# Two load queues, idle transposes, a second PSUM bank and another order of weight loads in a fused threshold-attention and MoE kernel

## Chip, cores, metric

One core of a Trainium2 chip. The metric is device microseconds of one execution. A trace covers the span from the first to the last instruction, which lies 1.8 us under the time of the same execution. "Mean clock" is the share of TensorE's full clock that the chip granted, averaged over the span; a "dip" is a stretch at half of it. One dip of 3.41 us takes 0.003 off the mean; half speed after the last matmul counts too, and takes up to 0.002.

## The reference

```python
def _attn_ref(q, k, v, tau):                 # q, k, v: (8, 8, 576, 64)
    scores = np.matmul(q, k.transpose(0, 1, 3, 2)) / np.sqrt(64)
    thresh = np.max(scores, axis=-1, keepdims=True) - tau
    scores = np.where(scores >= thresh, scores, -1000000000.0)
    attn = softmax(scores)
    return np.matmul(attn, v)
# heads side by side: x is (4608, 512)
def _moe_ref(x, w_in, w_out):                # (512, 2048), (2048, 512)
    h = x @ w_in
    return (h * np.clip(h + 3.0, 0.0, 6.0) / 6.0) @ w_out
```

## The kernel before

Heads come in quads (four heads, 16 quads), a quad in nine slots of score rows, so 144 slots. In each slot VectorE takes the row maximum out of PSUM, GpSimd makes a bias of it, ScalarE masks and takes the exponential, GpSimd normalizes, and a transpose (by DMA, or in early odd slots by TensorE) makes the operand for the product with v. From slot 23 on, pieces of the MoE run between the slots. What stands behind other work in an engine's line has to wait for it (the prediction shows GpSimd's bias behind three loads). The weights are loaded by GpSimd, in loads that also convert them to bf16. A bank, below, is a buffer in PSUM, the memory that TensorE writes its results to: the next product into it waits until it has been emptied.

```python
    N1 = 22
    N2 = 28
    ...
    def bank(name):                       # for transposes and products with v
        nonlocal turn
        turn += 1
        if now < N2 and turn % 2:
            return ps_o.tile([P, 512], F32, tag="o", name=name)   # ps_o: one bank, later MoE's
        return ps_m.tile([P, 512], F32, tag="m", name=name)       # ps_m: one bank
    ...
    def warm_up(count):                   # idle transposes: nobody reads the result
        warm = ps_h.tile([P, 2, 512], F32, tag="h", name="warm")
        for _ in range(count):
            nc.tensor.transpose(warm[:, 0, 0:P], identf[:], identf[:])
    ...
    transpose_rest(0)()                   # last of k and q of the first quad
    ...
    for n, sl in enumerate(queue):        # the slots
        ...
        if prev is not None:
            for i in range(2):
                sm_exp(prev, i)           # ScalarE
        sm_max(sl)                        # VectorE maximum, GpSimd bias
        ...                               # a piece of the MoE, reciprocal of prev
        for i in range(2):
            sm_mask(sl, i)                # ScalarE, waits for the bias
        ...                               # transposes, products with v
        if n + 1 < len(queue):
            queue[n + 1].tiles = scores(queue[n + 1].quad, queue[n + 1].slot)
        if n < 8:
            warm_up(6)
        if prev is not None:
            sm_norm(prev)                 # GpSimd
        flush()
        late.extend(outs)
        start(loads, 1)                   # q and k, on SyncE
        if n < 4 or n > 12:
            start(vcasts, 1)              # v, on GpSimd
        if n > 3:
            start(casts, 1 if n < 24 else 2)   # weights, on GpSimd
```

Of the kernel before, what the change touches and what calls it, by code (L numbers as in the profile page):

```python
# [9 lines left out]
F32 = mybir.dt.float32  # L10
# [3 lines left out]
Act = mybir.ActivationFunctionType  # L14

P = 128
# [5 lines left out]
def kernel(  # L22
# [10 lines left out]
    nc = tc.nc  # L33
    B, H, S, D = q.shape
    assert (B, H, S, D) == (8, 8, 576, 64)
    d_model, d_ff = moe_w_in.shape
# [4 lines left out]
    NSLOT = 9  # L41
    NB = 2
    N1 = 22
    N2 = 28
    scale = 1.0 / math.sqrt(D)
    tau = float(tau)

# [12 lines left out]
    o_pool = ctx.enter_context(tc.tile_pool(name="op", bufs=3))  # L60
# [14 lines left out]
    casts = []  # L75
# [4 lines left out]
    def load_quad(quad):  # L80
        b, g = divmod(quad, 2)
        nat[quad] = (nat_pool.tile([P, 1152], F32, tag="nq", name="nq"),
                     nat_pool.tile([P, 4, 4, D], F32, tag="km", name="km"),
                     nat_pool.tile([P, 2 * D], F32, tag="kr", name="kr"))
        nq, km, kr = nat[quad]

        def main(dst, src, h, order):
            nc.sync.dma_start(out=dst[:, :, h, :], in_=src[b, 4 * g + h, 0:512, :].rearrange(order, t=4))

        def blocks_q(n, a, j):  # L90
            c = 32 * (2 * a + j)
            nc.sync.dma_start(out=nq[c:c + 32, n * S:(n + 1) * S].rearrange("p (k d) -> p k d", d=32),
                              in_=q[b, 4 * g + 2 * n + a, :, 32 * j:32 * j + 32].rearrange("(k r) d -> r k d", r=32))

        def load_q(n):
            if b < NB:
                for a in range(2):
                    main(nq[:, 0:1024].rearrange("p (t h d) -> p t h d", h=4, t=4), q, 2 * n + a, "(t p) d -> p t d")
            else:
                for a in range(2):  # L100
                    for j in range(2):
                        blocks_q(n, a, j)

        def rest():
            for dst, src in ((kr[:], k), (nq[:, 1024:1152], q))[0:2 if b < NB else 1]:
                for n in range(2):
                    nc.sync.dma_start(out=dst[64 * n:64 * n + 64, :].rearrange("p (h d) -> p h d", h=2),
                                      in_=src[b, 4 * g + 2 * n:4 * g + 2 * n + 2, 512:S, :].rearrange("h p d -> p h d"))

        for n in range(2):  # L110
            loads.append(lambda n=n: [main(km, k, 2 * n + a, "(p t) d -> p t d") for a in range(2)])
            loads.append(lambda n=n: load_q(n))
            if n == 0:
                loads.append(rest)
# [34 lines left out]
    def start(jobs, n):  # L149
        for _ in range(min(n, len(jobs))):  # L150
            jobs.pop(0)()
# [9 lines left out]
    def warm_up(count):  # L161
# [3 lines that stand above are left out]
# [34 lines left out]
    def copy_out(out, in_):  # L199
        if 0 <= now < N1:  # L200
            nc.vector.tensor_copy(out=out, in_=in_)
        else:
            nc.scalar.copy(out=out, in_=in_)  # L203


    def by_pe(pair):
        return pair // NPAIR < NB
# [16 lines left out]
    def transpose_k(pair):  # L224
        ps = main_pe(nat[pair // 2][1], pair)
        return lambda: copy_out(kT_of(pair)[:, 64:576], ps[:])

    def transpose_rest(quad):
        ps = bank("tr")
        nq, _, kr = nat[quad]  # L230
        nc.tensor.transpose(ps[:, 0:P], kr[:], identf[:])
        if by_pe(2 * quad):
            nc.tensor.transpose(ps[:, P:2 * P], nq[:, 1024:1152], identf[:])

        def evict():
            qT, kT = qkT[quad]
            both = ps[:].rearrange("p (w n t) -> p w n t", n=2, t=64)
            if by_pe(2 * quad):
                nc.vector.tensor_copy(out=qT[:, :, 512:S], in_=both[:, 1])
            copy_out(kT[0:64, :, S:S + 64], both[0:64, 0])  # L240
            copy_out(kT[64:P, :, 0:64], both[64:P, 0])
        return evict

    def keys(pair, a, hf):
# [140 lines left out]
    def mm2_out(bb, mt, on_act):  # L385
        osb = o_pool.tile([P, d_model], F32, tag="osb", name="osb")
        if on_act:
            nc.scalar.activation(out=osb[:], in_=o_ps[0], func=Act.Copy, scale=1.0 / 6.0)  # L388
        else:
            nc.vector.tensor_scalar_mul(out=osb[:], in0=o_ps[0], scalar1=1.0 / 6.0)  # L390
        b0 = 2 * bb * S
        if mt == 4:
            return [(osb[0:64, :], out[b0 + 512:b0 + S, :]), (osb[64:P, :], out[b0 + S + 512:b0 + 2 * S, :])]
        r0, t = (b0, mt) if mt < 4 else (b0 + S, mt - 5)
        return [(osb[:], out[r0 + t * P:r0 + (t + 1) * P, :])]
# [23 lines left out]
    evict_q = transpose_q(0)  # L419
    evict()  # L420
    evict_q()
    transpose_rest(0)()

    queue = []
    for quad in range(NQUAD):
# [8 lines left out]
    for n, sl in enumerate(queue):  # L434
        quad, slot = sl.quad, sl.slot
        b, g = divmod(quad, 2)
        now = n
        if slot in (0, 4):
            pts[2 * quad + slot // 4] = pt_pool.tile([P, 9, 512], BF16, tag="pT", name="pT")
        if slot == 8:  # L440
            ptr[quad] = ptr_pool.tile([P, 9, P], BF16, tag="pR", name="pR")
        if quad == 0 and slot == 0:
            load_quad(1)
        if slot == (4 if quad else 8) and quad + 2 < NQUAD:
            load_quad(quad + 2)
        if slot == 0 and g == 1 and b + 1 < B:
            load_v(b + 1)
        if prev is not None:
            for i in range(2):
                sm_exp(prev, i)  # L450
        sm_max(sl)

        if slot != 8 and todo1:
            item, then = todo1.pop(0)
            h = mm1(item)
            r = mm1_relu(h, on_act=(slot in (0, 1, 3, 5)))
            mm1_gate(item, h, r)
            todo2.extend(then)
        copies = pe_transpose(queue[n - 2]) if n > 1 and queue[n - 2].on_chip else None
        if prev is not None:  # L460
            sm_recip(prev)
        if copies:
            copies()
        outs = []


        pieces = 0 if slot == 3 else 1
        if slot == 0:
            second = True
        if second and slot < 2 and len(todo2) > 1 and todo2[0][1] == todo2[1][1]:  # L470
            pieces, second = 2, False
        for _ in range(pieces):
            if todo2:
                bb, mt, part = todo2.pop(0)
                mm2_part(bb, mt, part)
                if part == 3:
                    outs += mm2_out(bb, mt, on_act=False)
        for i in range(2):
            sm_mask(sl, i)
        evict = None  # L480
        nxt = 2 * quad + 2
        if slot == (1 if quad else 2):
            evict = transpose_q(2 * quad + 1)
        elif slot == (2 if quad else 3):
            evict = transpose_k(2 * quad + 1)
        elif slot == 3 and quad > 0:
            av_main(2 * quad - 1)
        elif slot == 4 and quad > 0:
            av_rest(quad - 1)
            if quad % 2 == 0:  # L490
                todo1.extend(moe_of(quad // 2 - 1))
        elif slot in (5, 6, 7) and quad + 1 < NQUAD:
            if slot == 5:
                alloc_qk(quad + 1)
                evict = transpose_q(nxt)
            elif slot == 6:
                evict = transpose_k(nxt)
            else:
                evict = transpose_rest(quad + 1)
        elif slot == 8:  # L500
            av_main(2 * quad)
        if evict:
            evict()
        if n + 1 < len(queue):
            queue[n + 1].tiles = scores(queue[n + 1].quad, queue[n + 1].slot)
        if n < 8:
            warm_up(6)
        if prev is not None:
            sm_norm(prev)
        flush()  # L510
        late.extend(outs)
        start(loads, 1)
        if n < 4 or n > 12:
            start(vcasts, 1)
        if n > 3:
            start(casts, 1 if n < 24 else 2)
        prev = sl

    for i in range(2):
# [3 lines left out]


    last = NQUAD - 1
    count = [0, 0]

    def rest1(item, then):
        h = mm1(item, pool=ps_s if count[0] % 3 else None)
# [4 lines left out]
    def rest2():  # L534
        while todo2:
            bb, mt, part = todo2.pop(0)
            mm2_part(bb, mt, part, pool=ps_s if count[1] % 3 else None)
            if part == 3:
                flush()
                late.extend(mm2_out(bb, mt, on_act=(count[1] % 2 == 0)))  # L540
                count[1] += 1

    for item in todo1:
# [42 lines left out]
```

## Time and profile before

| | |
|---|---|
| three runs before the prediction | 561.0, 561.12, 562.59 us |
| the run that was profiled | 564.1 us (span 562.3, mean clock 0.989) |
| first mask, third, fourth (ScalarE, slots 0, 2, 3) | 10.72, 18.23, 21.31 us |
| mask of slot 14, of slot 31 | 54.80, 112.25 us |

The start of ScalarE's mask is a good milestone: one per slot, in order, on an engine that is 90% busy from 25 to 109 us (75.62 of 84 us). Compare two traces by the difference of these starts, slot by slot; it stays constant where nothing changed and steps where something did. The lines are in the prediction.

### The profile page before, as it was taken

What the parts mean: (1) busy time and instruction counts of PE and PEld (TensorE: products, weight loads), DVE (VectorE), ACT (ScalarE), POOL (GpSimd) and SP (SyncE); (2) the same over time, 40 slices, a digit from 0 to 9 for tenths busy, and PEclk for the clock granted to TensorE, in tenths of its full rate; (3) what the DMA queues carried; (4) which work ended last, traced back from release to release, by engine and by line L of the source; (5) the groups of instructions that cost most, each with busy time, mean ns of one, the idle gap of its engine ahead of it and who ended that gap; (6) DMA issues with size and microseconds to landing.
All of it is one profiled execution on the core that took longest, in us unless ns stands there. A gap on an engine that the chain in (4) does not pass through costs nothing.

```text
span 562.3 us, 11634 instructions
## 1 busy us (share of the span) xinstructions
PE 535.0 (95%) x3856; PEld 309.3 (55%) x3856; DVE 424.4 (75%) x1040; ACT 470.3 (84%) x999; POOL 305.2 (54%) x646
## 2 busy tenths in 40 slices
PE   7998798899999999999999999999999999999997
PEld 5665455455545565555555565655555565654663
DVE  3588787687878788787878798887978798883440
ACT  4799899798988999989898999899898999983540
POOL 1678878854556555655456555755556555561000
PEclk8899999899999999999999999999999999999999
DMA  5879999997689876978589867987699865453102
GB/s 110 135 110 166 162 160 184 207 148 144 112 159 153 151 153 127 208 139 155 114 150 170 159 137 146 174 160 146 127 137 175 167 124 117 101 109 86 38 20 75
DMA packets 286204, 77.52 MB, mean 138 GB/s; under 512 B 269248, under 2 KB 281536, under 8 KB 286144
## 3 DMA queue, kind: packets, MB, share of 16 engines
q1 hardware_dynamic: 268736, 67.86, 64.8%
q0 software_dynamic: 17408, 8.92, 13.7%
q8 instruction: 30, 0.49, 0.4%
q14 instruction: 30, 0.25, 0.2%
HBM read 36.70 MB, written 9.44 MB: 82 GB/s over the span
## 4 chain that ended last, share of the span: by engine, by line
PE 58%; DVE 11%; ACT 9%; issue 4%; POOL 1%; DMA 1%; SPq 1%; DVEq 0%; POOLq 0%
PE h L353 18%; PE o L382 17%; PE s L256 16%; DVE s L277 5%; ACT s L285 4%; PE av L323 3%; ACT s L290 3%; DVE g L370 2%; DVE r L364 2%; ACT r L362 2%; PE s L262 1%; PE tp L213 1%; PE ar L323 1%; DVE osb L390 1%; POOL pn L298 1%
## 5 line engine op out<-in xcount | busy, mean ns | idle before, releaser
L298 POOL TENSOR_SCALAR pn<-s,rinv 128x576 bf16<-128x576 f32 x288 | 211.6, 745 | 133.5 <-issue 58.5
L277 DVE TENSOR_SCALAR_CACHE_REDUCE s<-s 128x576 f32<-128x576 f32 x288 | 205.9, 752 | 44.9 <-PE s L256 35.2
L285 ACT ACTIVATE s<-s,bias 128x576 f32<-128x576 f32 x288 | 207.1, 766 | 36.8 <-POOL bias L280 35.7
L290 ACT ACTIVATE s<-s 128x576 f32<-128x576 f32 x288 | 192.7, 671 | 0.3
L256 PE MATMUL s<-kT,qT 64*128 64x288 f32 x1024 | 172.7, 435 | 5.4 <-DVE s L277 3.2
L353 PE MATMUL h<-xT,w_in_sb 128*128 128x320 bf16 (+1 forms) x1024 | 145.0, 287 | 5.5 <-DVE g L370 4.6
L382 PE MATMUL o<-w_out_sb,g 128*128 128x512 bf16 x576 | 140.9, 379 | 3.6 <-DVE osb L390 3.0
L353 PEld LDWEIGHTS <-w_in_sb 128*128 128x128 bf16 x1024 | 92.0, 97 | 68.4 <-issue 31.1
L256 PEld LDWEIGHTS s<-kT,qT 64*128 64x128 f32 x1024 | 94.8, 188 | 62.7 <-DVE s L277 24.9
L370 DVE SCALAR_TENSOR_TENSOR g<-r,h 128x512 bf16<-128x512 f32 (+1 forms) x128 | 96.4, 754 | 41.2 <-ACT r L362 39.3
L280 POOL TENSOR_SCALAR bias<-m 128x1 f32<-128x1 f32 x288 | 54.4, 189 | 69.0 <-DVE s L277 48.2
L382 PEld LDWEIGHTS <-g 128*128 128x128 bf16 x576 | 55.6, 98 | 58.2 <-issue 9.8
L362 ACT ACTIVATE r<-h,three 128x640 f32<-128x640 f32 (+1 forms) x74 | 54.4, 737 | 21.1 <-PE h L353 20.4
L290 ACT ACTIVATION_READ_ACCUMULATOR s<-s 128x1 f32 x288 | 54.2, 188 | 0.0
L364 DVE TENSOR_SCALAR r<-h 128x512 f32<-128x512 f32 (+1 forms) x54 | 40.5, 751 | 0.0
L390 DVE TENSOR_SCALAR osb<-o 128x512 f32<-128x512 f32 x31 | 21.0, 676 | 22.2 <-PE o L382 22.2
L323 PE MATMUL av<-pT,vm 128*64 128x512 bf16 x256 | 34.6, 392 | 2.0 <-ACT kT L203 2.0
L323 PEld LDWEIGHTS <-vm 128*64 128x64 bf16 x512 | 18.1, 111 | 25.2 <-issue 18.3
L293 DVE RECIPROCAL rinv<-rsum 128x2 f32<-128x2 f32 x144 | 23.0, 160 | 10.2 <-ACT s L290 9.5
L335 DVE CAST xT<-av 128x512 bf16<-128x512 f32 x32 | 21.8, 681 | 5.6 <-PE av L326 5.3
L277 DVE DVE_READ_ACCUMULATOR s<-s 128x1 f32 x288 | 23.9, 83 | 0.0
L388 ACT ACTIVATE osb<-o 128x512 f32<-128x512 f32 x5 | 3.0, 597 | 23.9 <-PE o L382 23.9
(42 smaller groups left out, 255.9 us busy)
## 6 DMA issues: line engine op xcount, KB each, us to landing
km<-in_k_dram SPq DMA_DIRECT2D x64, 128.0 KB, 3.0
out_dram<-osb SPq DMA_DIRECT2D x32, 256.0 KB, 2.4
nq<-in_q_dram SPq DMA_DIRECT2D x96, 72.0 KB, 2.7
vm<-in_v_dram POOLq DMA_DIRECT2D x16, 256.0 KB, 5.4
nq<-in_q_dram SPq DMA_DIRECT2D x16, 128.0 KB, 3.9
w_in_sb<-in_moe_w_in_dram POOLq DMA_DIRECT2D x16, 128.0 KB, 4.1
w_out_sb<-in_moe_w_out_dram POOLq DMA_DIRECT2D x16, 128.0 KB, 4.5
pT<-pn SPq DMA_TRANSPOSE x119, 3.4
```

The costliest lines, as they stand in the source:

```text
L256: nc.tensor.matmul(tiles[a][:, hf, 0:HALF], qT_of(pair)[a * 64:(a + 1) * 64, t * P:(t + 1) * P], keys(pair, a, hf), start=True, stop=True)
L277: nc.vector.tensor_scalar(out=sl.s[:, i, :].rearrange("p (a b) -> p a b", a=2), in0=ps[:, :, 0:HALF], scalar1=1.0, scalar2=None, op0=Alu.m ...
L280: nc.gpsimd.tensor_scalar(out=sl.bias[:, i:i + 1], in0=sl.m[:, i:i + 1], scalar1=-scale, scalar2=tau, op0=Alu.mult, op1=Alu.add)
L285: nc.scalar.activation(out=s, in_=s, func=Act.Prelu, bias=sl.bias[:, i:i + 1], scale=scale, alpha=REJECT)
L290: nc.scalar.activation(out=s, in_=s, func=Act.Exp, accum_out=sl.rsum[:, i:i + 1])
L298: nc.gpsimd.tensor_scalar(out=pn[:, i, :], in0=sl.s[:, i, :], scalar1=sl.rinv[:, i:i + 1], scalar2=1.0, op0=Alu.mult, op1=Alu.mult)
L323: nc.tensor.matmul(ps[a * 64:(a + 1) * 64, :], vm[:, 2 * hp + a, c * D:(c + 1) * D], pT[:, 5 * a + c, cols], start=(c == 0), stop=False)
L353: nc.tensor.matmul(hps[:, n, 0:w], w_in_sb[:, ki, (ni + n) * P:(ni + n + 1) * P], xT[b][:, ki, c0:c0 + w], start=(ki == 0), stop=(ki == KI ...
L362: nc.scalar.activation(out=r, in_=hps, func=Act.Relu, bias=three[:])
L364: nc.vector.tensor_scalar(out=r, in0=hps, scalar1=3.0, scalar2=0.0, op0=Alu.add, op1=Alu.max)
L370: nc.vector.scalar_tensor_tensor(out=gbuf[:, ni:ni + 2, c0:c0 + w], in0=r, scalar=6.0, in1=hps, op0=Alu.min, op1=Alu.mult)
L382: nc.tensor.matmul(o_ps[0], gbuf[:, ni, mt * P:(mt + 1) * P], w_out_sb[:, ni, :], start=(ni == 0), stop=(ni == NI - 1))
```

## The change

Its intent: get the first scores out sooner, keep TensorE's clock up in the lead-in, take weight loads out of slots 24 to 29 where the bias waits for them, spare a product with v the wait for a bank, and shorten the tail.

```diff
-    N2 = 28
+    N2 = 31
@@ load_q of the first quad, first pair: from ScalarE's queue
+                    main(..., by=nc.scalar if quad == n == 0 else nc.sync)
@@ transpose_rest(quad, of_k=True, of_q=True): does the k half, the q half or both
-    transpose_rest(0)()
+    transpose_rest(0, of_q=False)()
+    warm_up(6)
@@ in the slots
+        elif n == 1:
+            evict = transpose_rest(0, of_k=False)
+        if n == 0:
+            warm_up(8)
         if n + 1 < len(queue):
             queue[n + 1].tiles = scores(...)
-            start(casts, 1 if n < 24 else 2)
+            start(casts, 2 if n < 14 and n % 2 else 1)
@@ tail
-    count = [0, 0]
+    count = [1, 0]
+    def last_out():          # columns 0:256 by ScalarE, 256:512 by VectorE, a store on each queue
```

More of the change, by code (lines that the diff above doesn't have):

```diff
@@ L85, in load_quad, with main @@
         nq, km, kr = nat[quad]
-        def main(dst, src, h, order):
-            nc.sync.dma_start(out=dst[:, :, h, :], in_=src[b, 4 * g + h, 0:512, :].rearrange(order, t=4))
+        def main(dst, src, h, order, by=nc.sync):
+            by.dma_start(out=dst[:, :, h, :], in_=src[b, 4 * g + h, 0:512, :].rearrange(order, t=4))
         def blocks_q(n, a, j):
@@ L97, in load_q @@
                 for a in range(2):
-                    main(nq[:, 0:1024].rearrange("p (t h d) -> p t h d", h=4, t=4), q, 2 * n + a, "(t p) d -> p t d")
+                    main(nq[:, 0:1024].rearrange("p (t h d) -> p t h d", h=4, t=4), q, 2 * n + a, "(t p) d -> p t d",
+                         by=nc.scalar if quad == n == 0 else nc.sync)
             else:
@@ L226, in transpose_k, with transpose_rest @@
         return lambda: copy_out(kT_of(pair)[:, 64:576], ps[:])
-    def transpose_rest(quad):
+    def transpose_rest(quad, of_k=True, of_q=True):
         ps = bank("tr")
         nq, _, kr = nat[quad]
-        nc.tensor.transpose(ps[:, 0:P], kr[:], identf[:])
-        if by_pe(2 * quad):
+        of_q = of_q and by_pe(2 * quad)
+        if of_k:
+            nc.tensor.transpose(ps[:, 0:P], kr[:], identf[:])
+        if of_q:
             nc.tensor.transpose(ps[:, P:2 * P], nq[:, 1024:1152], identf[:])
@@ L237, in evict @@
             both = ps[:].rearrange("p (w n t) -> p w n t", n=2, t=64)
-            if by_pe(2 * quad):
+            if of_q:
                 nc.vector.tensor_copy(out=qT[:, :, 512:S], in_=both[:, 1])
-            copy_out(kT[0:64, :, S:S + 64], both[0:64, 0])
-            copy_out(kT[64:P, :, 0:64], both[64:P, 0])
+            if of_k:
+                copy_out(kT[0:64, :, S:S + 64], both[0:64, 0])
+                copy_out(kT[64:P, :, 0:64], both[64:P, 0])
         return evict
@@ L525 @@
     last = NQUAD - 1
-    count = [0, 0]
+    count = [1, 0]
+    def last_out():
+        osb = o_pool.tile([P, d_model], F32, tag="osb", name="osb")
+        r0, c = B * S - 64 - P, d_model // 2
+        nc.scalar.activation(out=osb[:, 0:c], in_=o_ps[0][:, 0:c], func=Act.Copy, scale=1.0 / 6.0)
+        nc.scalar.dma_start(out=out[r0:r0 + P, 0:c], in_=osb[:, 0:c])
+        nc.vector.tensor_scalar_mul(out=osb[:, c:2 * c], in0=o_ps[0][:, c:2 * c], scalar1=1.0 / 6.0)
+        nc.sync.dma_start(out=out[r0:r0 + P, c:2 * c], in_=osb[:, c:2 * c])
     def rest1(item, then):
@@ L539, in rest2 @@
                 flush()
-                late.extend(mm2_out(bb, mt, on_act=(count[1] % 2 == 0)))
+                if (bb, mt) == (B // 2 - 1, 8):
+                    last_out()
+                else:
+                    late.extend(mm2_out(bb, mt, on_act=(count[1] % 2 == 0)))
                 count[1] += 1
```

## The prediction

> **What bounds the kernel now.** I read the page first (busy shares, the 40 slices), then the chain of work that ended last, then the timelines of single engines and the busy time by stretch.
>
> ```profile
> PE 535.0 (95%) x3856; PEld 309.3 (55%) x3856; DVE 424.4 (75%) x1040; ACT 470.3 (84%) x999; POOL 305.2 (54%) x646
> PEclk8899999899999999999999999999999999999999
> ```
>
> TensorE is 95% busy: from about 109 us on it is the bound (29 to 30 us busy in each 30 us stretch to 500). The change touches none of its work there. What can move lies where TensorE is not the bound: the lead-in (0 to 25 us), the slots in which softmax alone sets the pace (25 to 109 us, one slot about 2.9 us, then 3.2 to 4.7), and the tail. The clock row shows a dip in the second slice; busy time by stretch places it:
>
> ```profile
> 9.64:10.96 1.32, 0.93 (x4) 0.29 (x2) 1.32 (x3) 0.24 (x1) 0.19 (x1) 0.99 1.03 233
> 10.96:17.62 6.66, 6.66 (x25) 4.07 (x24) 2.21 (x8) 5.42 (x12) 3.70 (x7) 0.50 0.38 56
> 106.96:109.24 2.28, 2.28 (x11) 0.89 (x10) 0.38 (x1) 2.28 (x6) 1.91 (x5) 0.50 1.29 192
> ```
>
> Behind the busy times of PE, PEld, DVE, ACT and POOL stands the granted clock: half speed for 6.66 us in the lead-in and again around 107 us. The TensorE timeline shows what that cost:
>
> ```profile
> 7.59 0.30 PE L233 MATMUL tr<-identf,nq 128*128 128x128 f32 x1 [0.81 <-DMA nq<-in_q_dram]
> 7.82 0.75 PE L256 MATMUL s<-kT,qT 64*128 64x288 f32 x2
> 8.83 1.23 PE L256 MATMUL s<-kT,qT 64*128 64x288 f32 x6 [0.27 <-ACT kT L203]
> 10.46 2.96 PE L256 MATMUL s<-kT,qT 64*128 64x288 f32 x8 [0.39 <-DVE s L277]
> 13.35 1.54 PE L164 MATMUL warm<-identf 128*128 128x128 f32 x6
> 14.82 2.29 PE L256 MATMUL s<-kT,qT 64*128 64x288 f32 x8
> ...
> 106.96 1.92 PE L323 MATMUL av<-pT,vm 128*64 128x512 bf16 x8 [2.03 <-ACT kT L203]
> ```
>
> The first scores wait for the transposed rest of q (7.59), whose load was the last of eight transfers on one queue, and then for a copy. Eight score records take 2.96 and 2.29 us cold; warm they take 1.24. At 106.96 the product with v stands 2.03 us, until ScalarE has emptied a bank, and then runs cold (1.92 against 1.05). ScalarE's timeline shows where it starves:
>
> ```profile
> 18.23 1.45 ACT L285 ACTIVATE s<-s,bias 128x576 f32<-128x576 f32 x2 [1.59 <-POOL bias L280]
> ...
> 101.08 1.44 ACT L285 ACTIVATE s<-s,bias 128x576 f32<-128x576 f32 x2 [1.39 <-POOL bias L280]
> ```
>
> and GpSimd's why it did at 101: the bias stands in line behind a load of v and two weight loads.
>
> ```profile
> 98.92 0.80 POOL L121 DMA_DIRECT2D vm<-in_v_dram  x1
> 99.72 1.07 POOL L146 DMA_DIRECT2D w_out_sb<-in_moe_w_out_dram  x2
> 100.87 0.46 POOL L280 TENSOR_SCALAR bias<-m 128x1 f32<-128x1 f32 x2
> ```
>
> In the tail, the last block of 80 matmuls waits for the gate of a hidden tile, since it takes over that tile's buffer:
>
> ```profile
> 540.81 17.43 PE L382 MATMUL o<-w_out_sb,g 128*128 128x512 bf16 x80 [0.62 <-DVE g L370]
> ```
>
> **What the Trainium skill says.** (1) "TensorE: Matmul & The Clock Gate", Part 1, What's actually happening: the clock is set by a free-running window of 3413 ns; too little work in one and it is halved. The trace agrees: the clock fell at 10.96 and at 106.5, and 95.5 us are 28.0 such windows; it came back at 17.6 (two windows) and 109.8 (one). As the phase is free, each run may draw another. (2) The same page, Part 4, PE-mode transpose, says that transposes do not count as activity for the clock. If so, idle transposes would be useless. The trace speaks against it: the weight loads of the first 14 transposes cover 2.82 us (0.20 each), those of the four at 5.83 cover 0.42 (0.10 each), with only transposes before them, so they did raise the clock. (3) "DMA: Bandwidth & Descriptors", Issuing engines are not separate DMA queues: a second issuing engine saves only the time to initiate. The trace agrees in so far as an issue on SyncE takes 0.55 to 0.70 us and the two key loads, the two query loads and the four small ones start one after the other up to 5.97 us.
>
> **The change, part by part.** The order of instructions confirms the diff: 14 more idle transposes, the q half of the first rest moved behind the second slot's scores, two loads moved to ScalarE's queue, five doubled weight loads early, a split last eviction.
>
> *Lead-in.* Moving two query loads takes 1.17 us off SyncE's line, so the small key load lands about 1.2 us earlier. But keys and queries now share the transfer (0.5 MB; at the 230 to 280 GB/s seen at 4 to 5 us about 2 us), so the first transposes may start 0.2 us later than 4.83. The rest of the keys is transposed at about 6.7, ScalarE's two copies (0.53) end at 7.4, the queries' eviction (0.69) at 7.4. So scores start near 7.5 without the wait for q, and the first maximum starts some 1.1 us later, at 8.7, not 9.64: 0.9 us gained. If the clock holds (6 + 8 idle transposes at 0.11 to 0.14 us fill 6.8 to 7.5 and 8.8 to 9.9), scores of slots 1 and 2 take 1.24 us each, ScalarE never starves and keeps its own 2.8 us per slot: the third slot's mask comes at 9.9 + 2 x 2.8 = 15.5, not 18.23. That is 2.7 us; if the clock falls all the same, 0.9. I give the clock 0.7: 0.7 x 2.7 + 0.3 x 0.9 = 2.2 us gained. The q half (0.27 us of VectorE, one transpose) lies beside other work.
>
> *Weight loads early.* One costs GpSimd 0.58 us. Five odd slots (5 to 13) get one more. GpSimd's slot is bias 0.46 + norm 1.41 + load 0.58 + gaps = 2.6 us; with two, 3.15; the mean of 2.88 is just under the 2.94 us that these slots took. Slot 13 has a v load as well and was already GpSimd-bound (ScalarE idle 0.60 there): it pays all 0.55. The other four I put at 0.2 each: 1.3 us lost.
>
> *Weight loads late.* Slots 24 to 29 lose one load (0.54). It counts where ScalarE waited for the bias: before the slots at 89.76 (idle 0.56), 101.08 (1.39) and 105.00 (1.14), at most 3 x 0.54 = 1.6. Slot 30 gets one it had not (up to 0.5 back). Some 1.1 gained.
>
> *Two banks up to slot 31.* The product at 106.96 need not wait for the key copy: it starts at 104.9 and warm. That is 2.03 of wait and some 1.4 of slow clock off TensorE. But ScalarE is busy without a gap from 105.00 to 111.5, and VectorE's next gate hangs on it (3.42 idle before 108.86), so the scores behind the product help only to where ScalarE's chain allows. On the chain, VectorE's maximum at 110.92 waited 0.71 for these scores, and TensorE leads from 106.96 to 121. I credit 1.2 beyond the ScalarE gain above.
>
> *Tail.* With the counter started at 1, the 21 hidden tiles of the tail take buffers one place further; the last block then inherits the buffer of the third-last tile, gated at 539.9, and starts at 540.2: 0.6 gained. The last eviction (0.60 for 512 columns) becomes two of 256 on two engines: by the step between 512 and 640 columns (0.69 to 0.79 us) some 0.4 each, 0.2 gained. The store moves the same 256 KB; its about 2.0 us to landing stay.
>
> Sum: 2.2 - 1.3 + 1.1 + 1.2 + 0.8 = 4.0 us. 561.1 - 4.0 = **557.1 us**. All of it arises before 109 us or after 524; between them TensorE just starts earlier.
>
> **Rivals.** (a) *The clock falls all the same.* The window's phase is free, score matmuls use 64 rows only, and windows that the trace counts as 80% busy were slow. Against it: the idle transposes fill the two gaps (8.57 to 8.83, 9.8 to 10.46) of just the window that failed. Then 1.3 us less than the sum: 558.4. (b) *GpSimd becomes the bound of slots 5 to 14*, as its 2.88 is so near 2.94 that each doubled load costs all 0.55: 2.75 lost, 558.5; added to (a), 559.9. For it: in this stretch most masks wait for the bias by 0.1 to 0.3 us. Against it: every other slot has slack. (c) *The late gains add in full*: TensorE alone sets the pace from 107 us and gets 3.4 rather than 1.2, with the loads' 1.6: 554.5. For it: the chain goes over TensorE from 106.96 on. (d) *ScalarE holds everything*: nothing of the second bank's gain, 558.3.
>
> **Range and chances.** (a), (b) and (d) together give 561, (c) with a held clock 554 or a little less. An 8-in-10 range is 554.3 to 559.8. 2% is 11.2 us, three times what the sum gives and more than all the named waits together: faster 0.02, same 0.97, slower 0.01.
>
> **What would show it.** Granted clock 1.00 from 8 to 25 us; first mask near 9.9 and third near 15.5 (10.72 and 18.23 before). ScalarE's idle before the masks of slots 6 to 14 grown by about 1.3 in sum. No bank wait of the v product in slot 30, and a clock of 1.00 around it. The last matmul block without its 0.6 of wait. TensorE's busy time in 30 us stretches from 120 to 500 unchanged. I am wrong if the clock still falls before 18 us, if slot 14 is reached no earlier than before, or if the gain at slot 31 is lost again later.

## The result, and the profile after

Measured: the changed kernel 560.92 us (median of 6, 559.91 to 562.67), the kernel before 562.65 (median of 6, 561.0 to 563.4). The ratio is 0.9977 (95% interval 0.9954 to 1.0). A ratio here is the mean time of one kernel's runs over that of the other's of the same rounds, so not quite the ratio of the medians. The predicted 557.1 (554.3 to 559.8) was too low by 3.8 us.

Yet the trace after looks as predicted. First, busy time by stretch of the changed kernel: busy us of PE, PEld, DVE, ACT, POOL, then the granted clock.

```profile
9.64:10.96 1.32, 1.32 (x9) 0.88 (x8) 0.57 (x2) 1.11 (x2) 0.78 (x3) 1.00 0.38 84
10.96:17.62 6.66, 6.60 (x51) 4.87 (x49) 5.37 (x16) 6.52 (x16) 5.32 (x11) 1.00 0.52 65
```

The clock holds at 1.00, and 51 matmul records fit where 25 did. TensorE's timeline in the lead-in and at the product with v:

```profile
7.50 1.24 PE L260 MATMUL s<-kT,qT 64*128 64x288 f32 x8
8.67 1.09 PE L165 MATMUL warm<-identf 128*128 128x128 f32 x8
9.69 1.81 PE L260 MATMUL s<-kT,qT 64*128 64x288 f32 x8
...
102.69 1.05 PE L327 MATMUL av<-pT,vm 128*64 128x512 bf16 x8
...
536.60 17.43 PE L386 MATMUL o<-w_out_sb,g 128*128 128x512 bf16 x78
```

Scores start at 7.50 without a wait, the product with v has lost its 2.03 us wait and the tail's block its 0.62. GpSimd's and ScalarE's timelines where the bias stood behind three loads:

```profile
96.84 0.80 POOL L122 DMA_DIRECT2D vm<-in_v_dram  x1
97.64 0.54 POOL L147 DMA_DIRECT2D w_out_sb<-in_moe_w_out_dram  x1
98.25 0.46 POOL L284 TENSOR_SCALAR bias<-m 128x1 f32<-128x1 f32 x2
```

```profile
53.24 1.44 ACT L289 ACTIVATE s<-s,bias 128x576 f32<-128x576 f32 x2 [1.27 <-POOL bias L284]
...
98.47 1.44 ACT L289 ACTIVATE s<-s,bias 128x576 f32<-128x576 f32 x2 [0.87 <-POOL bias L284]
```

The idle time before the mask of slot 28 fell from 1.39 to 0.87; before that of slot 14 it rose from 0.60 to 1.27, the price of the doubled loads.

The mask starts, changed minus before, from the two profiled runs:

| slot | 0 | 2 | 4 | 10 | 14 | 24 | 25 | 28 | 29 | 31 | 32 | 36 | 143 | end |
|---|---|---|---|---|---|---|---|---|---|---|---|---|---|---|
| us | -0.87 | -2.79 | -3.13 | -2.60 | -1.56 | -1.55 | -2.08 | -2.62 | -3.16 | -2.61 | -3.17 | -3.42 | -3.42 | -4.19 |

Between these two traces the change is worth 4.2 us, and the prediction's sum was 4.0. Between the two kernels' means it is worth 1.3. That the two traces differ by nearly the predicted sum is in part luck. The clock held in the lead-in, and with that the prediction's parts come to 4.5: 2.7 - 1.3 + 1.1 + 1.2 + 0.8. Measured are 3.13 up to slot 4, -1.57 to slot 14, 1.87 in slots 25 to 36 (1.1 + 1.2 predicted) and 0.77 in the tail. The larger fault lies in what the traces stand for: the profiled run of before took 564.1 us, that of after 559.91, the fastest of its six.

### The profile page after: what moved, and what is told of

Read it like the earlier page. It is cut to its first block, busy times and chain, and to the rows that moved or that the text cites. A ratio compares the mean times of both kernels' runs of the same rounds, so it can differ in the third digit from the quotient of the medians. Undisturbed runs are those within 1.5% of the kernel's fastest.

```text
span 558.1 us, 11625 instructions
## 1 busy us (share of the span) xinstructions
PE 529.1 (95%) x3829; PEld 308.6 (55%) x3870; DVE 424.6 (76%) x1041; ACT 469.4 (84%) x999; POOL 305.3 (55%) x646
## 4 chain that ended last, share of the span: by engine, by line
PE 54%; DVE 10%; ACT 10%; issue 4%; DMA 2%; POOL 2%; SPq 2%; DVEq 0%; POOLq 0%
PE h L357 17%; PE o L386 16%; PE s L260 14%; DVE s L281 4%; ACT s L289 4%; ACT s L294 4%; PE av L327 3%; DVE g L374 2%; ACT r L366 2%; DVE r L368 2%; DMA nq<-in_q_dram 2%; POOL pn L302 1%; PE tp L214 1%; PE s L266 1%; DVE osb L394 1%
## 5 line engine op out<-in xcount | busy, mean ns | idle before, releaser
L260 PE MATMUL s<-kT,qT 64*128 64x288 f32 x1024 | 169.7, 430 | 4.6 <-DVE s L281 2.8
L386 PE MATMUL o<-w_out_sb,g 128*128 128x512 bf16 x535 | 133.5, 379 | 5.2 <-DVE osb L394 3.0
L266 PE MATMUL s<-kT,qT 64*64 64x288 f32 x256 | 20.1, 415 | 0.7 <-DVE s L281 0.7
```

Of the source, the lines that this page charges most:

```text
L260: nc.tensor.matmul(tiles[a][:, hf, 0:HALF], qT_of(pair)[a * 64:(a + 1) * 64, t * P:(t + 1) * P], keys(pair, a, hf), start=True, stop=True)
L386: nc.tensor.matmul(o_ps[0], gbuf[:, ni, mt * P:(mt + 1) * P], w_out_sb[:, ni, :], start=(ni == 0), stop=(ni == NI - 1))
```

## The experiments

My theory (A) after the result: the window that sets TensorE's clock runs free of the kernel's start, so each execution draws its own dips; the profiled run of before had drawn 10.2 us of dips inside the span's working part, that of after none, and I had taken the cost of the dips off a time (561.1) of other runs that, by their times, had mostly not paid it (their clocks are not on record). Rival (B): the profile, or the chip, adds time that has nothing to do with the clock. Rival (C), from the skill's page that the prediction names: idle transposes do not hold the clock at all. In every job the kernel before ran on the same chip; its means in the three jobs were 562.42, 562.65 and 562.63 us (11 runs each).

### e1 and e2: both kernels again, with the clock of every run

e1 is the kernel before, e2 the changed one, both without an edit.

> The kernel before, unchanged, for the clock of each of its runs. Theory A (the clock's free phase): the profiled run of before (564.1 us, clock 0.989, two dips that cost) was an unlucky draw, and its trace was 2 to 3 us slower than a run without dips; then single runs spread over 561 to 564 us, the time falls as the run's granted clock rises, and a run at 0.996 or more is near 561.3. Rival B (the profile or the chip adds time that has nothing to do with the clock): no order between clock and time among the runs.

> The changed kernel, unchanged, on the same chip. Theory A: its runs also spread with the clock, from 559.9 (clock 1.0) to some 562.5 (0.990), the mean near 561.0, 1.3 us under the kernel before: the idle transposes hold the clock in only part of the runs. Rival B: the mean differs from the kernel before by the 4.2 us that the two traces differ by, so near 558.

e1: median 561.97; e2: median 560.52 (560.03 to 560.81), ratio to before 0.9963 (0.9951 to 0.9974). e2's runs did not spread as expected: none has a clock under 0.997. Its mean, 560.46, is far from rival B's 558. The runs of e1 and of the kernel before in that job, time and mean clock:

```
e1      561.19 0.999   561.47 0.998   561.52 0.997   562.42 0.995   563.56 0.993   563.81 0.992
before  561.21 0.999   561.44 0.998   561.99 0.995   562.18 0.993   562.39 0.995   562.66 0.990
        562.67 0.995   562.68 0.995   562.70 0.991   562.85 0.995   563.89 0.994
changed 559.91 1.000   560.61 0.997   560.63 0.999   561.22 0.992   561.29 0.992   562.67 0.990
```

(The last row is the first job's.) Time and clock go together: over 39 runs of the kernel before the correlation is -0.89, over the changed kernel's 12 it is -0.88. Runs of before at 0.997 or more have a mean of 561.6 us (16 runs), those under 0.994 one of 563.8 (10). Rival B falls as an account of these two kernels. The clock is not the only cause of spread, though: in e6 (below) the two slowest runs (563.26, 562.31) have higher clocks (0.996, 0.995) than the three fastest (0.994). And a correlation does not tell what a dip costs, since a wait can bring it along; two traces of one kernel do.

The phase is free, as theory A has it: in the twelve traces the clock first comes up anywhere from 4.10 to 7.32 us, and within each trace its changes lie whole multiples of 3.41 us apart.

e1's traced run happened to have no dip in the lead-in, though it is the same kernel as the first trace (busy time by stretch):

```profile
10.96:17.62 6.66, 6.66 (x44) 4.60 (x43) 4.43 (x14) 6.52 (x14) 4.91 (x11) 1.00 0.44 56
95.80:99.20 3.40, 3.40 (x17) 2.55 (x16) 2.27 (x7) 2.13 (x6) 3.32 (x6) 0.51 1.30 207
```

ScalarE's timeline, the masks of slots 2 and 3:

```profile
16.45 1.44 ACT L285 ACTIVATE s<-s,bias 128x576 f32<-128x576 f32 x2
19.15 1.44 ACT L285 ACTIVATE s<-s,bias 128x576 f32<-128x576 f32 x2
```

Here the clock is 1.00 to 17.62 and the third slot's mask comes at 16.45, not 18.23; the fourth at 19.15, not 21.31: so the dip in the first trace had cost 2.2 us. e1's own dip, at 95.8, cost nothing that its masks show. And e1 and e2, as it fell, are in the same state at the start (both cold until about 7 us: the clock came up at 7.09 and 6.74), and both have a dip of 3.41 us that begins near 95.6 (95.84 and 95.49), so their traces compare like with like: the spans are 559.7 and 558.8. The difference of their masks, e2 minus e1, is -0.40 at slot 4, +1.19 at slot 14, +0.86 at slot 24, -0.81 at slot 30, -0.2 from slot 31 to the last, and -0.93 at the end. (Of the step back at slots 20 to 22, e1 has 0.36 from a wait of GpSimd for a DMA transpose, which e2 does not have.) Of the parts, only the tail and some 0.2 us of the rest remain, when no dip that costs is in it.

### e3: without the added idle transposes

```diff
     transpose_rest(0, of_q=False)()
-    warm_up(6)
...
-        if n == 0:
-            warm_up(8)
```

> The changed kernel without the 6 and the 8 added idle transposes. Theory A: the clock falls in the lead-in in most runs, the third mask comes near 17.5 us in a trace with the dip, and the mean is 1.3 to 2 us above the changed kernel. Rival C (the idle transposes do nothing for the clock, as transposes do not count): the mean is within 0.4 us of the changed kernel, and clocks are spread alike.

Median 562.29 (559.78 to 562.81), mean 561.95 against e2's 560.46 on the same chip. Its fastest run, 559.78, is as fast as any of e2's (560.03); four of the other five had clocks of 0.990 to 0.996, where e2's lowest was 0.997. So the transposes cost nothing that the fastest runs show, and the runs with them are faster in the mean, by 1.5 us against e2 and by 1.2 against all twelve runs of the changed kernel (560.76). Three of those twelve, in the first job, had dips too (clocks 0.990 to 0.992), and that job's six alone are only 0.9 under e3, with ranges that overlap. That the added transposes bring fewer dips is likely, then; how much it is worth is known loosely.

Rival C falls on the traces. In all twelve of them the clock first rises before the first scores, when TensorE has run nothing but transposes. In e3's trace, TensorE's weight loads:

```profile
1.36 2.85 PEld L165 LDWEIGHTS warm<-identf 128*128 128x128 f32 x14 [1.36 <-POOL identf masks.py:199]
5.00 0.42 PEld L214 LDWEIGHTS tp<-identf,km 128*128 128x128 f32 x4 [0.78 <-issue]
```

They take 0.20 us each before the rise at 4.36 us and 0.10 after it. In the 3.41 us before the rise, transposes kept TensorE busy for 80 to 97% of the time (lowest and highest of the twelve traces); in the 3.41 us before those it was 0 to 74%, and the clock stayed down.

What held the clock later in the lead-in is not shown. The profiled run was the 559.78 one, which had drawn no dip, so the trace expected at 17.5 us for the third mask was not to be seen (it came at 15.26). Yet its windows lay almost as in the first trace. There TensorE was busy for 79% from 7.52 to 10.93 us, and the clock fell; here it was busy for 75% from 7.78 to 11.19, without the added transposes, and the clock stayed up. So the busy share did not tell which of these two windows fails, and the earlier scores may have been enough. No trace but the first has a dip before 55 us, e1's included.

### e4: the lead-in part alone

```diff
-    N2 = 31
+    N2 = 28
-            start(casts, 2 if n < 14 and n % 2 else 1)
+            start(casts, 1 if n < 24 else 2)
-    count = [1, 0]
+    count = [0, 0]
-                if (bb, mt) == (B // 2 - 1, 8):
+                if False:
```

> Only the lead-in part of the change (two queues, later q rest, idle transposes); weight loads, banks and tail as before. If the parts add, as the shifts of the mask times between the two traces say (lead-in 3.1 gained, early doubled weight loads 1.6 lost, slots 25 to 35 1.9 gained, tail 0.8 gained): this one is 0.9 to 1.3 us slower than the changed kernel at an equal clock, and its slot 14 is reached 1.6 us earlier than there. Rival: the lead-in's gain is absorbed later and the kernel takes the time of the kernel before.

Mean 561.35, e2's 560.46: 0.9 us slower, as expected, though not at an equal clock (0.995 to 0.997 against 0.997 to 1.0), and 1.1 us faster than the kernel before (ratio 0.9979, 0.9965 to 0.9992). In its trace slot 14 comes at 52.33 where e2 has 53.88, 1.55 us earlier from the same start: that is the cost of the doubled loads. ScalarE's timeline there:

```profile
48.95 1.44 ACT L289 ACTIVATE s<-s,bias 128x576 f32<-128x576 f32 x2
52.33 1.44 ACT L289 ACTIVATE s<-s,bias 128x576 f32<-128x576 f32 x2 [0.60 <-POOL bias L284]
```

### e5: the second bank given up at slot 28 again

```diff
-    N2 = 31
+    N2 = 28
```

> The changed kernel with the second bank given up at slot 28, as before. Theory A with the parts read from the traces: the late gain of slots 25 to 35 (1.9 us) is made of three saved weight loads (0.53 each, slots 25, 28, 29) and little else, since ScalarE is busy right through slots 29 to 31; the second bank is worth the dip in the clock behind its wait (0.8 us) in the runs that have it and 0.2 us in the others. So 0.2 to 0.6 us slower than the changed kernel. Rival, my prediction: 1.2 us slower.

The times (560.6 to 568.42, ratio to before 1.0014, 0.9976 to 1.0053) decide nothing: the clocks of the runs lie anywhere from 0.988 to 1.0, and one run, at 568.42, is 4.4 us above the next, which its clock (0.988 against 0.989) does not explain. That run stays open. The trace decides. TensorE's and ScalarE's timelines around slot 30:

```profile
106.70 1.05 PE L327 MATMUL av<-pT,vm 128*64 128x512 bf16 x8 [1.04 <-ACT kT L204]
```

```profile
106.09 0.56 ACT L204 COPY kT<-tp 128x512 f32<-128x512 f32 x1
107.90 0.67 ACT L366 ACTIVATE r<-h,three 128x512 f32<-128x512 f32 x1
108.47 1.43 ACT L289 ACTIVATE s<-s,bias 128x576 f32<-128x576 f32 x2
112.54 0.78 ACT L289 ACTIVATE s<-s,bias 128x576 f32<-128x576 f32 x1 [1.31 <-POOL bias L284]
```

The wait for the bank is back (1.04 us), and it costs nothing: the masks stand 2.24 us behind e2's in slot 24, 2.24 in slot 29, 2.24 in slot 31 and 2.24 in slot 40 (the constant is from the start and from a dip of 10.2 us at 55 us in this trace). ScalarE works on through slot 30, and the mask of slot 31 waits for GpSimd's bias (1.31 us), not for the scores behind the product with v. What the wait did cost in the first trace was the dip behind it: there slots 31 to 35 lost 0.8 us against e1. e4's trace, with the old bank too, has such a dip (105.67 to 109.09) and loses 1.0 us against e2 in the same slots. How often runs draw it was not measured.

### e6: the old order of weight loads

```diff
-            start(casts, 2 if n < 14 and n % 2 else 1)
+            start(casts, 1 if n < 24 else 2)
```

> The changed kernel with the old order of weight loads (one per slot to slot 23, then two). Theory A: slot 14 is reached 1.6 us earlier than in the changed kernel (no doubled load at slots 9, 11, 13), and slots 25, 28 and 29 lose 0.53 each again, so the move is worth nothing: within 0.4 us of the changed kernel. Rival: the early cost is real and the late gain not on the path, so 1 us or more faster than the changed kernel; or the other way round, 1 us slower.

Mean 561.19, median 560.61, ratio to before 0.998 (0.9957 to 1.0003): no difference from the changed kernel that the runs can tell. Its trace gives both sides: against e2 it is 1.59 us ahead in slot 14 relative to the start, loses 0.54 in slot 25, 0.53 in slot 28 and 0.54 in slot 29, and gains 0.61 in slot 31, where the changed order still has a weight load in the line before the bias. Together the changed order of loads costs about 0.5 us, leaving aside one wait for a DMA and a dip behind it at slots 21 and 22 of this trace (3.1 us), which the changed kernel's traces do not have.

### e7: the old tail

```diff
-    count = [1, 0]
+    count = [0, 0]
-                if (bb, mt) == (B // 2 - 1, 8):
+                if False:
```

> The changed kernel with the old tail (counter from 0, one eviction of 512 columns, one store). All theories: 0.75 us slower than the changed kernel (0.55 from the buffer order and the eviction, 0.2 from the store), with the last 80 matmuls waiting 0.6 us for a gate again. If it is within 0.2, the tail part was on no path.

From the last mask to the end of the span e7 took 58.20 us, e2 57.33: 0.87 slower in the trace. Of this, 0.79 arises before the last matmul ends. The mean, 561.90, is blurred by dips (one run at 0.989) and by another chip. The wait is back:

```profile
537.38 17.43 PE L386 MATMUL o<-w_out_sb,g 128*128 128x512 bf16 x80 [0.62 <-DVE g L374]
```

One thing in the new tail does not work as meant. The two halves of the last eviction run one after the other (changed kernel, timeline):

```profile
554.07 0.38 ACT L541 ACTIVATE osb<-o 128x256 f32<-128x256 f32 x1 [6.31 <-PE o L386]
...
554.48 0.42 DVE L543 TENSOR_SCALAR osb<-o 128x256 f32<-128x256 f32 x1 [3.12 <-ACT osb L541]
```

VectorE waits for ScalarE, and the eviction takes 0.84 us instead of 0.60. The last store, now of 128 KB, makes up for that: it landed 1.72 us after its issue, that of 256 KB (e7) after 2.00. So the gain of the tail is from the buffer order, and eviction and store together bring under 0.1 us. Whether a tile of its own for VectorE's half would remove the wait was not run.

### e8: weight loads in the lead-in

`gate` is a small GpSimd operation that reads the first transposed keys, so the three loads behind it start only then.

```diff
     warm_up(6)
+    gate = singles.tile([P, 1], F32, name="gate")
+    nc.gpsimd.tensor_scalar(out=gate[:], in0=kT_of(0)[:, 64:65], scalar1=1.0, scalar2=0.0, op0=Alu.mult, op1=Alu.add)
+    start(casts, 3)
...
-            start(casts, 2 if n < 14 and n % 2 else 1)
+            start(casts, 2 if n in (5, 7) else 1)
```

> A try at a version that beats both: three weight loads are issued in GpSimd's idle time before the first bias, gated on the first transposed keys so that they do not contend with the first q and k loads; then one load per slot but two in slots 5 and 7, where the trace shows that doubling cost nothing. Theory A: the 1.6 us lost by slot 14 comes back and the late gain stays, so 1.6 us faster than the changed kernel, near 558.9 us mean. If the three loads delay the q and k loads of the second pair, slots 2 to 4 come later and the gain is smaller.

Median 559.44 (558.24 to 562.7, 7 runs), ratio to before 0.9942 (0.9922 to 0.9963): 3.1 us under the kernel before in the mean, the best of all versions. The mean, 559.51, is 1.2 us under the changed kernel's twelve runs (on another chip); 558.9 was expected. Its lowest runs, 558.24 and 558.25, are 1.7 us under the changed kernel's lowest. GpSimd does the loads where it had nothing to do, and slot 14 is back at 52.43:

```profile
6.98 0.19 POOL L429 TENSOR_SCALAR gate<-kT 128x1 f32<-128x1 f32 x1 [5.67 <-ACT kT L204]
7.11 1.82 POOL L143 DMA_DIRECT2D w_in_sb<-in_moe_w_in_dram  x3
10.40 0.18 POOL L284 TENSOR_SCALAR bias<-m 128x1 f32<-128x1 f32 x1 [1.47 <-DVE s L281]
```

The profiled run was its slowest (562.7 us) and shows what can take the gain away. A transpose by DMA issued at 68.48 landed at 75.12, and the product with v of slot 21 waited for it, after which the clock dipped:

```profile
75.17 1.92 PE L327 MATMUL av<-pT,vm 128*64 128x512 bf16 x8 [1.99 <-DMA nq<-in_q_dram]
```

(The releaser named is the last landing before it; of the loads that the product needs, only transposes are so late.) Slot 22 came 3.6 us later than in e2, relative to slot 21; e6's trace loses 3.1 us in the same place. Why the transpose was late is not shown. Loads issued between 50 and 59 us took 5.8 to 8.7 us to land (3.1 is the median for keys in this trace), but they are as slow in the first trace (3.8 to 9.0) and in e2 (4.8 to 9.4). And of the traces that are in slot 14 as early, e6 and e8 have the wait while e4 (52.33) and e9 (52.15) have not: the faster slots alone do not bring it on.

### e9 and e10: idle transposes up to slot 21

```diff
-        if n < 8:
-            warm_up(6)
+        if n < 22:
+            warm_up(6 if n < 8 else 4)
```

e9 is this edit on e8, e10 on the changed kernel.

> The version with loads in the lead-in, with four idle transposes per slot also in slots 8 to 21, where traces of other draws had dips (10.2 us from 55 on, costing 1.9 us by slot 19; 3.4 us from 75 on). Theory A: fewer dips, so the runs lie closer together and the mean falls by 0.5 to 1 us against the same version without them (559.5 there), lowest run unchanged near 558.2. If the transposes stand in the way of score matmuls, every run is slower, lowest included, by up to 1 us.

> The changed kernel with four idle transposes per slot in slots 8 to 21. Theory A: no run at a clock of 0.992 or less from dips in this stretch; the lowest run stays at 559.9, the mean near 560.3. Rival: the spread of the changed kernel's runs (559.9 to 562.7) has another cause, and stays.

e9: median 560.06 (559.24 to 561.64), ratio 0.9957 (0.9931 to 0.9983). e10: median 561.01 (560.14 to 561.51), ratio 0.9971 (0.9949 to 0.9993). The long dips are gone: no run of the twelve has a clock under 0.997 (one of e9 is at 0.997, which leaves room for a dip of 3.41 us), and the spread fell, as theory A has it. The rest of what I expected did not come: both lowest runs rose, by 1.0 us for e9 over e8's and by 0.2 for e10, and the means, 560.15 and 560.94, did not fall (559.51 for e8, 560.76 for the changed kernel, each on another chip). In e10's trace slots 20 to 22 lose 0.49 us against e2: the transposes stand in line before products and scores. (e9's trace loses another 0.84 at slots 32 to 35; in it a product with v waits 1.65 us, up to 109.37, for a DMA transpose. Whether the edit brings that on, one trace does not tell.) In these runs, holding the clock in slots 8 to 21 was not worth its price.

## Why the prediction was wrong, point by point

- **The failed step: "561.1 - 4.0 = 557.1".** The 4.0 was read from a trace of a run that took 564.1 us with dips of 6.83 and 3.41 us in it; the 561.1 was from other runs. The dips' cost, 2.2 us in the lead-in (e1 against the first trace) and 0.8 around slot 31, was taken off runs that had not paid it. The table in my hands had both times, 3.0 us apart, and I passed over it. The like-for-like gain without dips that cost is 0.93 us (e2 against e1), 0.36 of it e1's wait for a DMA; in the mean, dips counted as they come, it is 562.53 - 560.76 = 1.8 us (39 runs of before, 12 of the changed kernel). So of the 3.7 us between 557.1 and 560.76, 1.4 come from the start, 561.1, which three runs had given too low, and 2.2 from a gain of 1.8 in place of 4.0.
- **Lead-in without the clock: 0.9 predicted.** 0.87 between the first traces (clock up at 4.10 and 5.26 us), 0.40 between e1 and e2 (up at 7.09 and 6.74): right in one pair, half of it in the other. The first mask goes with the time at which the clock comes up: of the ten traces with the new lead-in, four have it up by 5.3 us and the mask at 9.67 to 9.98, six from 6.48 on and the mask at 10.39 to 10.86.
- **The clock: held with probability 0.7, worth 1.8 more.** That a dip in the lead-in is paid is right: it cost 2.2 us in the run that had it, where 1.8 was predicted. That the added transposes are what kept it away there is not shown (e3), nor that they filled the gaps that mattered; in the mean the runs with them are 1.2 to 1.5 us faster, wherever their dips lay. What I had missed is that the other kernel draws too: the gain is the difference of two chances, not a dip removed. (A small misreading: the trace has the clock back at 17.75 and 109.91 us, not 17.6 and 109.8.)
- **Early weight loads: 1.3 lost.** 1.55 to 1.6 (e4, e6, e8). The mechanism was right, and the size for slot 13; the doubles in slots 5 and 7 were free, those in 9 and 11 cost 0.53 each, not 0.2, as rival (b) had it for all.
- **Late weight loads: 1.1 gained.** 1.6 in slots 25, 28 and 29, minus 0.6 in slot 31 for the load still to be issued in slot 30: 1.0. Right.
- **The second bank: 1.2 gained.** Nothing, without a dip (e5); 0.8 to 1.0 with one behind the wait (first trace, e4). Rival (d) was right, and I had its evidence: ScalarE without a gap from 105.00 to 111.5.
- **Tail: 0.8 gained.** 0.87 in the trace (e7), 0.74 between e1 and e2: right in size, though the split eviction lost 0.24 where I had it gain 0.2, the smaller last store gained 0.28, and 0.79 arose before the last matmul ended, where I had 0.6.

## What to carry to other kernels

Before a gain is read off a trace, compare the traced run's own time and clock with those of the other runs: a time and a trace may be different draws, and a cost seen once is to be weighed by how often it is drawn. A wait that ends on one engine is worth nothing if another engine is busy right through it; look there first. Work that an engine issues on the side belongs where that engine waits anyway (here 8 us before the first bias). And one trace of a faster version can hold a wait that other runs do not have (3.6 us in e8's): look at the runs' times before it is called the price of the change.

## What the Trainium skill lacked or had wrong

- "TensorE: Matmul & The Clock Gate", Part 4, PE-mode transpose, says that transposes do not count as activity for the clock. Here f32 transposes against an identity do: in all twelve traces the clock rose with nothing but them before it (at 4.10 to 7.32 us), and a weight load of theirs went from 0.20 to 0.10 us (e3).
- The same page, Why this matters for your kernels, warns of idle gaps over some 3 us. Here the clock fell at 10.93 us with no gap over 0.39 us in the 3.4 us before, and at 75.1 (e8) and 106.5 us in waits of 2.0 us: shorter gaps are enough. (Elsewhere the page has frequent short idle times do it, without a length.)
- The free phase of the window, from Part 1 of that page, agrees: dips lasted 3.41, 6.83 or 10.24 us. The page has it change the number of cold matmuls at a kernel's start from run to run. It does not say that dips anywhere in a tuned kernel then go with its spread: 561.0 to 565.8 us over 39 runs, correlated with the clock at -0.89.
- "DMA: Bandwidth & Descriptors", Anatomy of one DMA, has a fixed 2 us plus a rate for DMAs that GpSimd issues, by which 256 KB would take some 2.6 us (an estimate from the page's fit). It has no such fit for SyncE and ScalarE: here a last store of 256 KB landed 2.00 us after its issue on SyncE (e7), halves of 128 KB 1.72 (SyncE) and 1.75 us (ScalarE) after theirs. Nor has it a figure for crowded queues: loads of 128 KB took up to 8.7 us to land when issued at 55 us in e8.
